# Hash attention and a gated feed-forward on one core: another order of both stages' pools, and DMA landings counted in the planned order of the queues

## Chip, cores and metric

The kernel runs on one core of a Trainium2 chip. The metric is the device time of one execution in microseconds (us), as the median of several runs. All durations of single instructions come from one profiled execution.

## What is computed

The reference is a block of attention with a hash mask, followed by a feed-forward block:

```python
q, k, v: (4, 8, 768, 64)        proj: (64, 6)
q_bucket, k_bucket = buckets of (q @ proj > 0), (k @ proj > 0)   # 6 bits each
scores = where(q_bucket == k_bucket, q @ k.T / sqrt(64), -1e9)
attn   = exp(scores - max); attn /= attn.sum(-1) + 1e-9
x      = (attn @ v) as (3072, 512)
h      = x @ w_in               # w_in (512, 2048)
out    = (h * erf(softplus(h))) @ w_out      # w_out (2048, 512)
```

## The kernel before

**Two stages.** `attention` works on 16 pairs of heads. For pair i TensorE computes the scores (line 554, 12 blocks of 384 queries by 128 keys for each of the two heads), ScalarE takes the exponential (line 581), VectorE adds blocks up for the divisor (line 627, `sum_keys`), and TensorE multiplies by v (line 639, `weigh`). `feed_forward` then takes six tiles of 512 tokens. Both of its matrix products are done as seven block products in place of eight (a scheme of Strassen's kind), so VectorE makes sums of blocks beforehand: of x (line 343, `presum_x`), of w_in (line 796, `presum_weights`) and of w_out (line 1330, `presum_w`). The first product is at line 1245, its results are copied to the tiles `h` by ScalarE (line 1263, `read`) and added to by VectorE (line 1267, `complete`), a gate of sigmoids follows (lines 1275 to 1300), and the second product is at line 1358. For the first three of its 48 steps the first product uses PSUM banks that the second product doesn't need yet (names M in the profile), later the bank X.

**The order is written by a planner.** Each stage gives its steps to `arrange` as `Op` records: engine, cost, rank, what it comes after, and `late`, the time from the end of a step until its result can be used on another engine. `arrange` runs a simple model of the engines and returns one list. The instructions are issued in that order, so each engine's queue keeps it. The planner decides only the order. What is waited for in the run is set by semaphores, which follow from the data and from the memory that tiles share.

**The way of a pair's divisor.** `divisor` (line 684, TensorE) sums over the keys, `keep_divisor` copies to `z` (ScalarE), `spread` sends z to memory (SP, zd<-z, line 724), `gather` reads it back across the partitions (SP, zc<-zd, line 731), `invert` takes the reciprocal (VectorE, lines 741 and 744), `ungather` sends it out (SP, rd<-zc, line 749), `widen` reads it back broadcast (SP, r<-rd, line 759), `normalise` multiplies (VectorE, line 770) and `send` stores x (SP, xs<-x, line 778). The last pair, number 15, does this inside the feed-forward's list (`late`), with tiles in `area`.

**The way of a pair's bits.** `bits_of` (line 842, TensorE), `sign_of` (line 851, ScalarE), `weigh_bits` (line 861, VectorE), `leave_bits` (POOL, bd<-sg, line 871), `place_bits` (POOL, both<-bd, line 880). POOL also issues the loads of the weights in pieces (`fetch_weights`, raw<-in_w, line 460), which VectorE and ScalarE convert (lines 474 to 536). Three raw buffers take turns.

**The seam between the stages.** The pools of `attention` are closed when those of `feed_forward` open, and take the same memory from the same start. A pool lies behind the one opened before it. Before the change the bytes per partition, counted from that start, are:

| stage | pools in order |
|---|---|
| attention | load 0 to 27648, bitp to 34560, ep to 53808, xst 53824 to 72256, rawp to 84544, cvt |
| feed_forward | work 0 to 32768, hp to 65536, sums to 71680, wtp to 83968, outp |

The pool xst holds the tiles x, z and r of the divisor's way. The pool hp holds the eight tiles `h`. The first product of feed-forward starts with P1 and P2 (8 matmuls each); P6, the next, writes into the bank of P1 and so follows the copy of P1 to `h` (the first line 1263), then comes P5. P6, P5, P7 and P4 take sums that `presum_x` makes from the x of tile 0, loaded by `load_x(0)` (SP, area<-xs, line 331).

Of the kernel before, what the change touches and what calls it, by code (L numbers as in the profile page):

```python
# [86 lines left out]
class Op:  # L87
# [10 lines left out]
    free: tuple = ()  # L98
    table: str = None
    late: float = 0.06  # L100


TABLE_LOAD = 1.28
# [14 lines left out]
def arrange(ops, rooms, patience=0.0):  # L118

    names = {op.name: op for op in ops}
    users, missing = {}, {}
    for op in ops:
        needs = {a for a in op.after if a in names}
        missing[op.name] = len(needs)
        for a in needs:
            users.setdefault(a, []).append(op)
    ranked = sorted(ops, key=lambda op: op.rank)
    clock = {op.engine: 0.0 for op in ranked}  # L130
    ready, released = {}, {}
    rings = {ring: [] for ring in rooms}
    open_ops = {engine: [] for engine in clock}
    table = "exp"
    order = []

    def open_up(op):
        at = 0.0
        for a in op.after:
            if a in names:  # L140
                away = 0.0 if names[a].engine == op.engine else names[a].late
                at = max(at, ready[a] + away)
        open_ops[op.engine].append((op, at))

    def start_of(op, at):
        at = max(at, clock[op.engine])
        if op.take:
            ring, room = rings[op.take[0]], rooms[op.take[0]]
            if len(ring) >= room:
                at = max(at, released.get(ring[-room], float("inf")))  # L150
        return at

    for op in ranked:
        if not missing[op.name]:
            open_up(op)
    while len(order) < len(ops):
        best = None
        for engine, entries in open_ops.items():
            starts = [(start_of(op, at), op) for op, at in entries]
            starts = [each for each in starts if each[0] < float("inf")]  # L160
            if not starts:
                continue
            first = min(start for start, _ in starts)
            start, op = min(
                (
                    (start, op)
                    for start, op in starts
                    if start <= first + (patience if op.rank[0] == 0 and engine != "PE" else 0.0)
                ),
                key=lambda each: (each[1].rank, each[0]),  # L170
            )
            if best is None or start < best[0]:
                best = start, op
        start, op = best
        end = start + op.cost
        if op.table and op.table != table:
            table = op.table
            end += TABLE_LOAD
        clock[op.engine] = ready[op.name] = end
        if op.take:  # L180
            rings[op.take[0]].append(op.take)
        for what in op.free:
            released[what] = end + op.late
        open_ops[op.engine] = [each for each in open_ops[op.engine] if each[0] is not op]
        order.append(op)
        for user in users.get(op.name, ()):
            missing[user.name] -= 1
            if not missing[user.name]:
                open_up(user)
    return order  # L190
# [3 lines left out]
def kernel(  # L194
# [14 lines left out]
    NPAIR = B * H // 2  # L209
# [4 lines left out]
    JP = NPAIR // B  # L214
# [202 lines left out]
    def attention():  # L417
        NS = NPAIR * 4
        with (
            tc.tile_pool(name="load", bufs=3) as load,  # L420
            tc.tile_pool(name="bitp", bufs=1) as bitp,
            tc.tile_pool(name="ep", bufs=1) as ep,
            tc.tile_pool(name="xst", bufs=1) as xst,
            tc.tile_pool(name="rawp", bufs=3) as rawp,
            tc.tile_pool(name="cvt", bufs=1) as cvt,
            tc.tile_pool(name="psum", bufs=1, space=PSUM) as psum,
# [394 lines left out]
            def op(fn, args, engine, cost, rank, after=(), **more):  # L821
                name = (fn.__name__,) + args
                ops.append(Op(name, engine, cost, rank, lambda: fn(*args), after=after, **more))
# [93 lines left out]
            for what, n in order:  # L917
                free = slots[-3] if len(slots) >= 3 else ()
                if what == "score":
                    i = n // 4  # L920
# [57 lines left out]
            for h in range(NH):  # L978
                i = h // 2
# [3 lines left out]
            for i in range(NPAIR):  # L983
                n = 4 * i
                if i:
                    op(
                        start_pair,
                        (i,),
                        "SP",
                        3.6,  # L990
                        (0, n - 6),
                        (("weigh", n - 9), ("bits_of", i - 1))
                        + tuple(("measure", i - 3, m, half) for m in range(2) for half in range(2)),
                        late=3.5,
                    )
                    if i == 1:
                        op(place_first, (), "ACT", 0.9, (0, n - 2, 9), (("bits_of", i),))
                        for ab in (1, 0):
                            op(weigh_first, (ab,), "DVE", 0.43, (0, n - 2, 1), (("place_first",),))
                        op(double_first, (), "DVE", 0.35, (0, n - 2, 2), (("weigh_first", 0), ("weigh_first", 1)))  # L1000
                    else:
                        op(sign_of, (i,), "ACT", 0.6, (0, n - 6, 9), (("bits_of", i), ("leave_bits", i - 1)))
                        op(weigh_bits, (i,), "DVE", 0.33, (0, n - 6, 1), (("sign_of", i),))
                        op(leave_bits, (i,), "POOL", 0.7, (0, n - 6, 2), (("weigh_bits", i),), late=3.6)
                        op(
                            place_bits,
                            (i,),
                            "POOL",
                            1.2,
                            (0, n - 6, 3),  # L1010
                            (("leave_bits", i), ("score", n - 5, 2), ("clean", i - 2)),
                            late=3.6,
                        )
                for m in range(2):
                    for half in range(2):
                        op(
                            measure,
                            (i, m, half),
                            "ACT",
                            0.65,  # L1020
                            (1, 2 * i + 2, 2 + m, half),
                            (("start_pair", i), ("score", n, 0)),
                        )
                if i == NPAIR - 1:
                    continue
                op(spread, (i,), "SP", 0.4, (0, n, 0), (("keep_divisor", i),), late=3.0)
                op(gather, (i,), "SP", 0.35, (0, n, 1), (("spread", i),), late=4.5)
                op(invert, (i,), "DVE", 0.4, (0, n + 8, 3), (("gather", i),))
                op(ungather, (i,), "SP", 0.35, (0, n, 2), (("invert", i),), late=3.0)
                op(  # L1030
                    widen,
                    (i,),
                    "SP",
                    1.1,
                    (0, n, 3),
                    (("ungather", i), ("normalise", i - 2)),
                    late=6.5,
                )
                op(normalise, (i,), "DVE", 1.02, (0, n + 8, 4), (("widen", i), ("leave", 2 * i + 1)))
                op(send, (i,), "SP", 0.35, (0, n, 4), (("normalise", i),), late=2.2)  # L1040
            for n in range(2):
                op(clean, (n,), "POOL", 1.4, (0, 4 * n), (("score", 4 * n + 3, 2),), late=0.3)
            for n in range(len(pieces)):
# [7 lines left out]
                    late=7.0,  # L1051
# [7 lines left out]
            for k in range(4):  # L1059
# [11 lines left out]
                    )  # L1071
                    + ((("sum_keys", NPAIR - 1, 2),) if k % 4 == 3 else ()),
                )
            op(load_x, (0,), "SP", 1.1, (1, 0), (("send", JP - 1), ("divisor", NPAIR - 3)), late=4.0)
            for k in range(4):
                op(presum_x, (0, k), "DVE", 0.62, (2, 31, 8 + k), (("load_x", 0), ("presum_x", 0, k - 1), ("divisor", NPAIR - 2)))
            for each in arrange(ops, {}):
# [120 lines left out]
    def feed_forward(check, late):  # L1198
        again = late is None
        with (  # L1200
            tc.tile_pool(name="work", bufs=1) as work,
            tc.tile_pool(name="hp", bufs=8) as hp,
            tc.tile_pool(name="sums", bufs=1) as sums,
            tc.tile_pool(name="wtp", bufs=2) as wtp,
            tc.tile_pool(name="outp", bufs=1) as outp,
            tc.tile_pool(name="ps_f", bufs=1, space=PSUM) as ps_f,
            tc.tile_pool(name="ps_l", bufs=1, space=PSUM) as ps_l,
        ):
# [216 lines left out]
            def op(name, engine, cost, rank, fn, args, **more):  # L1425
                ops.append(Op(name, engine, cost, rank, lambda: fn(*args), **more))
# [277 lines left out]
            if late:  # L1704
                for k, (engine, cost, name) in enumerate(
# [10 lines left out]
                        late=6.0,  # L1716
# [53 lines left out]
    with tc.manual_schedule():  # L1770
        late = attention()
        feed_forward(judge, late)
    again = nc.values_load(flag[0:1, 0:1], min_val=0, max_val=1)
    with tc.If(again > 0):
        general()
        feed_forward(None, None)
# [53 lines left out]
```

## Time and profile before

| what | value |
|---|---|
| median of 3 runs (lowest, highest) | 910.35 us (909.51, 911.08) |
| profiled execution, its own time | 910.26 us |
| span of the profile | 908.2 us, so 2.1 us lie around it |
| mean granted TensorE clock | 0.995 of full speed |
| TensorE (PE) busy | 897.4 us, 99% of the span |
| VectorE (DVE) busy | 669.5 us, 74% |
| ScalarE (ACT) busy | 563.3 us, 62% |
| GpSimd (POOL) busy | 58.3 us, 6% |

A busy figure is the sum of the instructions' durations on one engine. In the views by windows each row is a stretch of the execution, with the busy time of each engine and the number of instructions in brackets, then the granted TensorE clock, the busy share of the DMA engines and GB/s. In the views of waits a row is who waited, for whom, and then the total in us, how often, and the longest. In a timeline a row has the start, the duration, the engine and the instructions, merged where equal ones follow each other.

### The profile page before, as it was taken

What the parts mean: (1) busy time and instruction counts of PE and PEld (TensorE: products, weight loads), DVE (VectorE), ACT (ScalarE), POOL (GpSimd) and SP (SyncE); (2) the same over time, 40 slices, a digit from 0 to 9 for tenths busy, and PEclk for the clock granted to TensorE, in tenths of its full rate; (3) what the DMA queues carried; (4) which work ended last, traced back from release to release, by engine and by line L of the source; (5) the groups of instructions that cost most, each with busy time, mean ns of one, the idle gap of its engine ahead of it and who ended that gap; (6) DMA issues with size and microseconds to landing.
All of it is one profiled execution on the core that took longest, in us unless ns stands there. A gap on an engine that the chain in (4) does not pass through costs nothing.

```text
span 908.2 us, 12781 instructions
## 1 busy us (share of the span) xinstructions
PE 897.4 (99%) x5016; PEld 673.2 (74%) x5016; DVE 669.5 (74%) x837; ACT 563.3 (62%) x808; POOL 58.3 (6%) x95
## 2 busy tenths in 40 slices
PE   9999999999999999999999999999999999999997
PEld 5455554455445578888888888888888888888886
DVE  5999999999989759996666556756776556655653
ACT  7788887788876548854645545555655555545520
POOL 1211211111210000000000001000100000000000
PEclk9999999999999989999999999999999999999999
DMA  9556665656652412201032114211321123011321
GB/s 232 148 141 174 174 180 159 179 165 176 155 176 60 128 62 64 82 35 70 30 88 81 35 47 105 82 35 47 87 99 35 35 58 93 35 30 50 73 70 50
DMA packets 65156, 86.82 MB, mean 96 GB/s; under 512 B 34364, under 2 KB 47772, under 8 KB 65088
## 3 DMA queue, kind: packets, MB, share of 16 engines
q1 hardware_dynamic: 56528, 63.81, 24.4%
q0 software_dynamic: 8112, 21.66, 8.4%
q8 instruction: 41, 0.67, 0.3%
q10 hardware_dynamic: 448, 0.46, 0.2%
q14 instruction: 27, 0.22, 0.1%
HBM read 64.67 MB, written 17.30 MB: 90 GB/s over the span
## 4 chain that ended last, share of the span: by engine, by line
PE 96%; DVE 2%; DMA 1%; issue 0%; ACT 0%; SPq 0%; ACTq 0%; DVEq 0%
PE M L1358 32%; PE X L1245 29%; PE st L554 16%; PE av L639 13%; PE M L1245 3%; PE bits L842 1%; PE bits L684 1%; DMA zd<-z 1%; PE warm L804 0%; DVE area L627 0%; PE bits L374 0%; DMA xs<-x 0%; PE z_ps L684 0%; DMA zc<-zd 0%; DVE x L770 0%
## 5 line engine op out<-in xcount | busy, mean ns | idle before, releaser
L1285 DVE SCALAR_TENSOR_TENSOR e<-w,e 128x1024 f32<-128x1024 f32 x144 | 173.7, 1220 | 8.3 <-ACT w L1279 3.9
L1245 PE MATMUL X<-area,w_in_sb 128*128 128x256 f32 x680 | 160.6, 379 | 0.0
L1279 ACT ACTIVATE w<-h,cq 128x1024 f32<-128x1024 f32 x144 | 155.6, 1136 | 0.1
L554 PE MATMUL st<-q,k 64*128 64x384 f32 x768 | 155.1, 482 | 0.0
L1267 DVE TENSOR_TENSOR h<-X,h 128x512 f32<-128x512 f32 x65 | 44.8, 689 | 144.4 <-PE X L1245 144.4
L1245 PEld LDWEIGHTS X<-area,w_in_sb 128*128 128x128 f32 x680 | 129.2, 190 | 17.6
L1358 PE MATMUL M<-w_out_sb,h 128*128 128x256 f32 x576 | 141.1, 379 | 0.0
L1245 PE MATMUL X<-area 128*128 128x256 f32 x520 | 122.8, 379 | 0.0
L1358 PEld LDWEIGHTS M<-w_out_sb,h 128*128 128x128 f32 x576 | 109.4, 190 | 14.9
L1263 ACT COPY h<-X 128x512 f32<-128x512 f32 x85 | 49.3, 580 | 111.4 <-PE X L1245 111.3
L1245 PEld LDWEIGHTS X<-area 128*128 128x128 f32 x520 | 98.8, 190 | 13.4
L1275 ACT ACTIVATE e<-h,cq 128x1024 f32<-128x1024 f32 x48 | 55.1, 1149 | 85.9 <-DVE h L1267 85.8
L1358 PE MATMUL M<-wt,S 128*128 128x256 f32 x384 | 95.1, 379 | 0.0
L554 PEld LDWEIGHTS st<-q,k 64*128 64x128 f32 x768 | 68.9, 187 | 29.2 <-issue 26.5
L627 DVE TENSOR_TENSOR area<-area 128x1536 f32<-128x1536 f32 (+1 forms) x46 | 79.5, 1729 | 3.5 <-ACT area L581 1.4
L1358 PEld LDWEIGHTS M<-wt,S 128*128 128x128 f32 x384 | 73.0, 190 | 9.9
L581 ACT ACTIVATE e_even<-st 128x768 f32<-128x768 f32 x96 | 70.5, 823 | 0.3 <-PE st L554 0.3
L581 ACT ACTIVATE area<-st 128x768 f32<-128x768 f32 x90 | 67.8, 817 | 0.0
L639 PE MATMUL av<-e_even,v 128*64 128x385 f32 x384 | 65.6, 490 | 0.0
L554 PE MATMUL st<-both 64*128 64x384 bf16 x384 | 63.6, 323 | 0.3 <-ACT both L387 0.3
L1300 DVE TENSOR_TENSOR h<-h,e 128x1024 f32<-128x1024 f32 x48 | 57.9, 1220 | 4.6 <-ACT e L1296 4.6
L639 PE MATMUL av<-area,v 128*64 128x384 f32 x360 | 60.6, 486 | 0.0
(129 smaller groups left out, 981.8 us busy)
## 6 DMA issues: line engine op xcount, KB each, us to landing
wt<-wt SPq DMA_DIRECT2D x24, 768.0 KB, 4.3
raw<-in_w_out_dram POOLq DMA_DIRECT2D x16, 512.0 KB, 4.7
raw<-in_w_in_dram POOLq DMA_DIRECT2D x14, 512.0 KB, 4.6
v<-in_v_dram SPq DMA_DIRECT2D x32, 192.0 KB, 3.9
q<-in_qkT_dram SPq DMA_DIRECT2D x30, 192.0 KB, 4.0
k<-in_qkT_dram SPq DMA_DIRECT2D x30, 192.0 KB, 4.4
r<-rd SPq DMA_DIRECT2D x30, 192.0 KB, 3.5
xs<-x SPq DMA_DIRECT2D x15, 384.0 KB, 2.8
```

What stands on the lines that cost most here:

```text
L554: nc.tensor.matmul(out=st[:, ab, 0:HS], lhsT=d["k" + src][rows, keys], rhs=d["q" + src][rows, cols], start=(part == 0), stop=(part == 1),)
L581: nc.scalar.activation(out=e[:, :, 0:HS], in_=st[:, :, 0:HS], func=AF.Exp, scale=scale)
L627: nc.vector.tensor_tensor(out=into, in0=one, in1=two, op=ALU.add)
L639: nc.tensor.matmul(out=d["av", half][rows, 0:w], lhsT=d["v"][:, g * GC + c, rows], rhs=e[:, ab, 0:w], start=(g == 0 and c == 0), stop=(g = ...
L1245: nc.tensor.matmul(out=d[where][:, u, :], lhsT=a[:, kc, f : f + P], rhs=b[:, kc, :], start=(first and u == 0 and kc == 0), stop=(last and ...
L1263: nc.scalar.copy(out=quarter(p, q), in_=st[p][where])
L1267: nc.vector.tensor_tensor(out=h, in0=st[p][where], in1=h, op=ALU.add)
L1275: nc.scalar.activation(out=s, in_=unit(p, v), func=AF.Sigmoid, bias=cq[:, n : n + 1])
L1279: nc.scalar.activation(out=q, in_=unit(p, v), func=AF.Sigmoid, scale=GATE_S[j][0], bias=cq[:, j : j + 1])
L1285: nc.vector.scalar_tensor_tensor(out=s, in0=st[p].pop(("q", v, j)), scalar=GATE_S[j][2], in1=s, op0=ALU.add, op1=ALU.mult,)
L1300: nc.vector.tensor_tensor(out=h, in0=h, in1=st[p].pop(("s", v)), op=ALU.mult)
L1358: nc.tensor.matmul(out=banks[name][:, sub, :], lhsT=a[:, u, sub * P : (sub + 1) * P], rhs=b[:, u, :], start=(c == 0 and k == 0), stop=(c = ...
```

## The change

It has four parts.

1. In `attention` the pool xst is opened after load and ahead of bitp and ep. In `feed_forward` the pools outp and sums are opened after work and ahead of hp and wtp. The sizes stay.
2. `Op` gets `far` and `near`. A step with `far=True` has its `late` counted for a user on the same engine too, unless the user names it in `near`. It is set for `leave_bits`, `spread`, `gather` and `ungather`, each followed by another transfer of the same queue that needs its data.
3. The values of `late` move: `leave_bits` 3.6 to 4.0, `spread` 3.0 to 3.5, `widen` 6.5 to 5.0.
4. `load_x(0)` comes after `gather` of pair 14 in place of `divisor` of pair 13, with `late` 6.5 in place of 4.0.

```diff
@@ class Op
     late: float = 0.06
+    far: bool = False
+    near: tuple = ()
@@ arrange, open_up
-                away = 0.0 if names[a].engine == op.engine else names[a].late
+                near = names[a].engine == op.engine and (not names[a].far or a in op.near)
+                away = 0.0 if near else names[a].late
@@ attention
             tc.tile_pool(name="load", bufs=3) as load,
+            tc.tile_pool(name="xst", bufs=1) as xst,
             tc.tile_pool(name="bitp", bufs=1) as bitp,
             tc.tile_pool(name="ep", bufs=1) as ep,
-            tc.tile_pool(name="xst", bufs=1) as xst,
@@
-    op(leave_bits, (i,), "POOL", 0.7, (0, n - 6, 2), (("weigh_bits", i),), late=3.6)
+    op(leave_bits, (i,), "POOL", 0.7, (0, n - 6, 2), (("weigh_bits", i),), late=4.0, far=True)
@@
-    op(spread, (i,), "SP", 0.4, (0, n, 0), (("keep_divisor", i),), late=3.0)
-    op(gather, (i,), "SP", 0.35, (0, n, 1), (("spread", i),), late=4.5)
+    op(spread, (i,), "SP", 0.4, (0, n, 0), (("keep_divisor", i),), late=3.5, far=True)
+    op(gather, (i,), "SP", 0.35, (0, n, 1), (("spread", i),), late=4.5, far=True)
     op(invert, (i,), "DVE", 0.4, (0, n + 8, 3), (("gather", i),))
-    op(ungather, (i,), "SP", 0.35, (0, n, 2), (("invert", i),), late=3.0)
+    op(ungather, (i,), "SP", 0.35, (0, n, 2), (("invert", i),), late=3.0, far=True)
@@ widen
-                    late=6.5,
+                    late=5.0,
@@
-    op(load_x, (0,), "SP", 1.1, (1, 0), (("send", JP - 1), ("divisor", NPAIR - 3)), late=4.0)
+    op(load_x, (0,), "SP", 1.1, (1, 0), (("send", JP - 1), ("gather", NPAIR - 2)), late=6.5, near=(("gather", NPAIR - 2),))
@@ feed_forward
             tc.tile_pool(name="work", bufs=1) as work,
+            tc.tile_pool(name="outp", bufs=1) as outp,
+            tc.tile_pool(name="sums", bufs=1) as sums,
             tc.tile_pool(name="hp", bufs=8) as hp,
-            tc.tile_pool(name="sums", bufs=1) as sums,
             tc.tile_pool(name="wtp", bufs=2) as wtp,
-            tc.tile_pool(name="outp", bufs=1) as outp,
```

## The prediction

> **What bounds the kernel now.** I read the engines' shares first, then who TensorE waits for, then the granted clock by stretches around the only long wait, and last the chain that leads into that wait. The page's first part:
>
> ```profile
> PE 897.4 (99%) x5016; PEld 673.2 (74%) x5016; DVE 669.5 (74%) x837; ACT 563.3 (62%) x808; POOL 58.3 (6%) x95
> ```
>
> TensorE is the bound. So only TensorE's idle time and its slow time can be won. All its waits, from the view of waits for PE:
>
> ```profile
> PE M L1245 <- ACT h L1263: 2.9, 1, 2.9
> PE warm L804 <- DVE ones L250: 1.0, 1, 1.0
> PE M L1245 <- DVE h L1267: 0.7, 1, 0.7
> PE st L554 <- ACT both L387: 0.3, 1, 0.3
> ```
>
> One wait matters: 2.9 us, once, in the first product of feed-forward, for the copy of a result to `h`. The windows around it, with the clock behind the bracketed counts:
>
> ```profile
> 313.43:317.15 3.72, 3.72 (x18) 2.96 (x16) 3.72 (x5) 0.48 (x1) 0.00 (x0) 1.00 0.40 134
> 317.15:320.09 2.94, 0.00 (x1) 0.00 (x0) 2.39 (x4) 0.59 (x1) 0.00 (x0) 0.85 0.34 134
> 320.09:326.65 6.56, 6.56 (x16) 5.04 (x17) 1.97 (x4) 0.59 (x1) 0.00 (x0) 0.55 0.30 121
> 326.65:347.70 21.05, 20.39 (x109) 17.02 (x109) 16.06 (x25) 14.45 (x18) 0.00 (x0) 1.00 0.09 26
> ```
>
> The reader is to see the third row: a "busy" TensorE that does 16 matmuls in 6.56 us, where 8 take 1.73 us later (a row of the long chain: `358.82 1.73 PE X L1245 x8`). The wait costs twice, as idle time and as a slow clock after it. Cut finer:
>
> ```profile
> 319.00:319.20 0.20, 0.00 (x0) 0.00 (x0) 0.20 (x1) 0.00 (x0) 0.00 (x0) 0.96 0.00 0
> 319.20:319.40 0.20, 0.00 (x0) 0.00 (x0) 0.20 (x1) 0.00 (x0) 0.00 (x0) 0.50 0.00 0
> 325.80:326.00 0.20, 0.20 (x2) 0.20 (x1) 0.00 (x0) 0.00 (x0) 0.00 (x0) 0.50 0.00 0
> 326.00:326.20 0.20, 0.20 (x3) 0.17 (x2) 0.00 (x0) 0.00 (x0) 0.00 (x0) 0.97 0.00 0
> ```
>
> The clock halves about 2.0 us after TensorE's last modelled end (317.15) and returns 5.9 us after it starts again. The chain of waits over this stretch says what the copy waited for:
>
> ```profile
> 315.49 1.02 DVE x L770
> 316.50 0.02 issue
> 316.52 2.30 DMA xs<-x
> ...
> 319.45 0.60 ACT h L1263
> 320.05 0.04 issue
> 320.09 6.63 PE M L1245 x16
> ```
>
> The copy of P1 could have started when P1's matmuls ended, near 315.4 (313.43 plus 8 matmuls, 1.73, plus about 0.2). It started at 319.45, behind the store of the last x that `normalise` made. No data joins them. What joins them is memory: hp covers bytes 32768 to 65536, and the tiles x lie at 53824 to 63040, in xst. The first tile h lies at 32768 to 36864 and touches no x, so the wait holds for the pool as a whole. The view of the tile x agrees (who waited for it: `ACT h L1263: 5.4, 1`).
>
> **What the skill says.** The Trainium skill, "TensorE: Matmul & The Clock Gate", Part 1: The HAM clock gate, says that TensorE's clock is halved after an idle window and restored after a busy one, and that the windows (about 3.4 us) run freely. The trace agrees on the half (0.50), with 2.0 us of idle time and 5.9 us of work around it. So a remaining wait under some 2 us need not halve the clock: the 0.66 us wait at 344.31 did not (clock 1.00 from 339 to 345). "DMA: Bandwidth & Descriptors", Issuing engines are not separate DMA queues, says that transfers of SP and POOL share the same engines. That bears on the reordered transfers; the trace has the DMA engines busy 0.56 of the time from 27.3 to 318.9.
>
> **The change part by part.**
>
> *Pools.* By the sizes in front of the reader, xst now lies at 27648 to 46080, bitp to 52992, ep to 72240. In feed-forward outp lies at 32768 to 45056, sums to 51200, hp at 51200 to 83968. So hp lies over both1, junk, e_even and the raw buffers, and no longer over x, z or r. What the first copy to `h` must now wait for: the exponentials' sums over e_even (DVE, done by about 304), the last squares into junk (ACT, 307.7 in the trace), the bits of pair 15 (landed by 287.4) and P1 itself. P1 is last. xst is now under work, outp and sums. Their first writers are the sigmoid at line 1275 (331.92 before, some 326 after), line 1315 and the output, all after the last store has landed (316.52 + 2.30 = 318.8). The four L1330, which waited 0.5 us for the store, are freed too. Price of the pools elsewhere: nothing, since no instruction changes its shape.
>
> *The gain.* From the start of P1 to the start of the next kind of work (z_ps, line 684) the trace has 326.65 - 313.43 = 13.22 us. The same 32 matmuls at 1.73 us per 8 take 6.92, and the changeover about 0.1. The gain is 13.22 - 7.0 = **6.2 us**: some 3.1 of idle time and 3.1 of half clock.
>
> *Does it last?* From 347.7 to 862 TensorE is busy 514.30 of 514.30 us, so whatever starts sooner ends sooner. Between 326.65 and 347.7 the order on TensorE, ScalarE and VectorE is the same in both programs, and everything there follows from TensorE's results. VectorE could be late instead: before, it idles 7.48 us ahead of line 1267 at 329.54. With TensorE 6.2 us sooner that line comes at 323.3. VectorE's work before it (the end of attention near 316.2 as worked out below, 2.5 for four L1330, 0.7 for the first line 1267) ends near 319.4, so 3.9 us are left. What is late next is the 0.66 us wait at 344.31, which stays.
>
> *The list.* TensorE's order is the same instruction for instruction. On SP `send` of pair i-1 now stands between `spread` and `gather` of pair i; before it stood ahead of both. At the end of attention, SP has spread 13, spread 14, send 12, gather 13, gather 14, load_x, ungather 13 and 14, widen 13 and 14. Worked out: `invert` of pair 12 comes one sum later (286.62 + 1.7 = 288.3), its r lands near 294.5, `normalise` 12 ends near 298, so send 12 goes at 298, the gathers at about 299, load_x at 299.7. In the trace load_x took from 295.42 to 301.28, 5.9 us, so x is there at 305.6. VectorE starts the last pair's sums at 300.3 (fourth exponential); 1.75 + 1.70 + 0.96 of sums, 0.8 of inverting, 1.23 at line 796, 1.9 of sums bring the first `presum_x` to 308.6 and the second, which P6 needs, to an end at 309.9. P6 could start at 316.9: 7 us to spare. The last sums end near 314.2 and `normalise` near 316.2, against 316.5 before. All of this lies beside TensorE. I take nothing for it. The bounds: not below nothing, since TensorE waits for none of this work now, and +1.5 above, the case of rival 1.
>
> *POOL.* One or two fetches (0.57 us each to issue) now stand between `leave_bits` and `place_bits`. The tightest pair before:
>
> ```profile
> 203.66 0.55 POOL L871 DMA_DIRECT2D bd<-sg  x1 [15.22 <-DVE sg L861]
> 208.99 1.16 POOL L880 DMA_DIRECT2D both<-bd  x2 [4.78 <-DMA bd<-sg]
> ```
>
> It lands 2.1 us later, at 212.25, and the scores that read it start at 219.23: 7.0 us of slack. A fetch fills the time in which POOL waited anyway (4.78 us). Sharing engines with a 512 KB piece costs at most its 4.7 us. I take nothing.
>
> The sum: 910.26 - 6.2 = 904.06 for the profiled execution, whose own time is 0.09 under the median. Prediction **904.1 us**.
>
> **Rivals.**
>
> 1. *A shorter wait takes its place.* P6 then waits for `presum_x`, as load_x stands behind the gathers and send 12. For: SP is strictly in order, and `normalise` 12 waits for a chain of four transfers. Against: 7 us of slack. If it comes 1.5 us too late the clock stays up: 904.1 + 1.5 = 905.6.
> 2. *The same loss by another way.* x lands 10 us later than worked out, P6 waits 3 us and the clock halves again: 910.3, no change. A form of it is that the pool still waits for the store by another tile; against it speaks that hp and xst no longer share a byte.
> 3. *Slower: bits too late.* A fetch stuck on a raw buffer holds `place_bits` on POOL. Its buffer is freed by a conversion on VectorE, 0.42 + 0.69 + 0.69 + 0.43 + 0.69 + 0.69 = 3.6 us, and ahead of it can stand a pair's five sums, 8.7 us. That is 12.3 us, 5.3 beyond the slack, and the idle TensorE then pays the half clock as well (3.1): 8.4 for each pair hit, 904.1 + 8.4 = 912.5 with one pair, 921 with two. It decides from a delay of 7 us. For: VectorE is busy 270.6 of 291.6 us in this stage. Against: on VectorE the conversion that frees the buffer stands ahead of the `weigh_bits` for which `leave_bits` has waited, in all but the earliest pair.
>
> **How the numbers follow.** The measurement can tell 0.2% (1.8 us) from no change. Forecast 0.87, rival 1 0.05, rival 2 0.04, rival 3 0.04. The forecast's own range is 903.2 to 905.2 (the runs before spread by 0.8 to each side, the gain by 0.3). Taken up to rival 1, and down for the 0.66 us wait at 344.31 going too, the range is 902.8 to 906.0. Faster 0.92, same 0.04, slower 0.04.
>
> **What would show it.** Right: no row "PE M L1245 <- ACT h" over 0.3 us, a clock of 1.00 from 313 to 345, the first copy to `h` near 315.5, z_ps near 320.4 in place of 326.65, and a span near 902. Wrong: a halved clock after 313, a wait of PE for `area` at line 343, or a wait of the scores for `both` with POOL behind a raw buffer.

## The result, and the profile after

| | median | lowest to highest | runs |
|---|---|---|---|
| before | 909.51 us | 907.82 to 911.08 | 5 |
| after | 904.56 us | 904.18 to 904.86 | 5 |

The ratio is 0.9945 (95% interval 0.993 to 0.9959): faster by about 5 us. The profiled execution of after took 904.72 us, with a span of 902.9 and a mean granted clock of 0.998 (before 910.26, 908.2 and 0.995). In the changed file every line touched here stands three lines lower, so L1263 is now L1266.

TensorE's waits in the kernel after, from the view of waits (who, for whom, then total, times, longest):

```profile
PE warm L807 <- DVE ones L253: 1.0, 1, 1.0
PE M L1248 <- DVE h L1270: 0.7, 1, 0.7
PE st L557 <- ACT both L390: 0.3, 1, 0.3
```

The 2.9 us row is gone and the three others are as they were. The timeline of TensorE at the seam of the two stages, after:

```profile
313.46 3.72 PE L1248 MATMUL M<-area,w_in_sb 128*128 128x256 f32 x16
317.02 3.62 PE L1248 MATMUL M<-area 128*128 128x256 f32 x16
320.56 0.86 PE L687 MATMUL z_ps<-area,ones 128*32 128x192 f32 x16
...
338.22 3.72 PE L1248 MATMUL M<-area,w_in_sb 128*128 128x256 f32 x16 [0.66 <-DVE h L1270]
```

The second row is P6 and P5. They follow P1 and P2 without a gap and take 3.62 us where they took 6.63. The windows over the same stretch give the granted clock, the third number from the end, as 1.00:

```profile
313.46:317.02 3.56, 3.56 (x19) 3.15 (x17) 3.51 (x5) 1.07 (x2) 0.00 (x0) 1.00 0.23 91
317.02:320.56 3.54, 3.54 (x17) 2.85 (x15) 2.40 (x4) 0.59 (x1) 0.00 (x0) 1.00 0.60 240
```

From P1 to `z_ps` there are now 320.56 - 313.46 = 7.10 us, against 13.22: 6.12 less, and the last matmul of the program ends 6.09 sooner (896.20 for 902.29). The span shrank by only 5.3, since the end behind the last matmul took 6.7 us in this execution and 5.9 in that of before. The timeline of all engines after, around the moved steps:

```profile
297.65 0.42 SPq L781 DMA_DIRECT2D xs<-x  x1
299.12 0.46 SPq L334 DMA_DIRECT2D area<-xs  x1
...
308.48 1.41 DVE L346 TENSOR_TENSOR area<-area 128x512 f32<-128x512 f32 x2
...
314.35 1.94 DVE L773 SCALAR_TENSOR_TENSOR x<-x,ev,r 128x768 f32<-128x768 f32 x2
315.38 1.25 SPq L781 DMA_DIRECT2D xs<-x  x2
315.61 0.59 ACT L1266 COPY h<-M 128x512 f32<-128x512 f32 x1 [1.56 <-PE M L1248]
...
323.45 0.69 DVE L1270 TENSOR_TENSOR h<-M,h 128x512 f32<-128x512 f32 x1 [4.03 <-PE M L1248]
```

The two stores of x in the row at 315.38 are issued at 315.38 and 316.31. The first copy to `h` starts at 315.61, so 0.70 us before the last store is even issued: it waits for TensorE, no longer for a store.

### The profile page after: what moved, and what is told of

Its sections match the earlier page's. It is cut to its first block, busy times and chain, and to the rows that moved or that the text cites. A ratio compares the mean times of both kernels' runs of the same rounds, so it can differ in the third digit from the quotient of the medians.

```text
span 902.9 us, 12780 instructions
## 1 busy us (share of the span) xinstructions
PE 894.3 (99%) x5016; PEld 670.9 (74%) x5016; DVE 668.5 (74%) x837; ACT 563.3 (62%) x808; POOL 57.9 (6%) x95
## 4 chain that ended last, share of the span: by engine, by line
PE 99%; DVE 0%; issue 0%; ACT 0%; DVEq 0%
PE M L1361 32%; PE X L1248 29%; PE st L557 17%; PE av L642 14%; PE M L1248 3%; PE bits L845 1%; PE bits L687 1%; PE warm L807 0%; PE bits L377 0%; PE z_ps L687 0%; DVE e L1288 0%; DVE h L1270 0%; ACT both L390 0%; DVE u L1396 0%; DVE norms L1754 0%
## 5 line engine op out<-in xcount | busy, mean ns | idle before, releaser
L1270 DVE TENSOR_TENSOR h<-X,h 128x512 f32<-128x512 f32 x65 | 44.8, 689 | 144.4 <-PE X L1248 144.4
L1266 ACT COPY h<-X 128x512 f32<-128x512 f32 x85 | 49.3, 580 | 111.4 <-PE X L1248 111.3
```

The lines of the kernel that those rows point to most:

```text
L1266: nc.scalar.copy(out=quarter(p, q), in_=st[p][where])
L1270: nc.vector.tensor_tensor(out=h, in0=st[p][where], in1=h, op=ALU.add)
```

## The experiments

The edits are given in short form here: a line that starts with # is a remark, and only what matters of each line is kept. In brackets behind a measured time stand its ratio to before and the 95% interval of the ratio.

**Two edits alone (e1, e2).** Both pool orders without the list's edits, and the list's edits without the pools. The list's edits are parts 2 to 4 of the change:

```diff
 # e1: before, and
-  pools load, bitp, ep, xst   /  work, hp, sums, wtp, outp
+  pools load, xst, bitp, ep   /  work, outp, sums, hp, wtp
 # e2: after, with the two pool orders of before
```

> The kernel before with the two pool orders of the change alone; every queue's order stays that of before. My theory (the whole gain is the wait of the first copy to h, and the slow clock after it): the copy starts at once after P1, the clock stays at 1.00, z_ps starts near 320.5, time 904.5 us, within 0.5 of the changed kernel. Rival (the list shares in the gain, because the sums of x or the stores come sooner with it): a wait of TensorE of 0.5 to 3 us stays at P6, time 905 to 910 us.

> The changed kernel with both pool orders of before: only the order of the queues is changed. My theory: the first copy to h waits for the last store of x as before. That store goes out some 0.2 us sooner, so the wait shrinks by 0.2 us at most, the clock is halved again, and the time is that of before, 909 to 910 us. Rival (the list carries part of the gain): 905 to 908 us.

Measured beside the same runs of before (910.95 us): pools 906.41 (ratio 0.9962, 0.9948 to 0.9975), list 910.96 (1.0004, 0.9994 to 1.0013). The list alone gives nothing; its profile has the old stall, from the timeline of TensorE of the list alone:

```profile
320.31 6.74 PE L1248 MATMUL M<-area 128*128 128x256 f32 x16 [3.05 <-ACT h L1266]
```

The pools remove it, but stop 1.8 us short of the 904.56 that the whole change had in another comparison. The expectation of 904.5 us was missed, and its rival did not come either: P6 has no wait, and P1 to `z_ps` takes 7.10 us as in the kernel after. In the profile of the pools alone VectorE stands still where the divisors come back, and TensorE has two short waits in the stage of attention. The timeline there:

```profile
193.85 0.17 DVE L741 TENSOR_SCALAR zc<-zc 128x12 f32<-128x12 f32 x1 [2.61 <-DMA zc<-zd]
...
194.21 5.35 DVE L627 TENSOR_TENSOR area<-area 128x1536 f32<-128x1536 f32 x3
...
199.48 0.15 DVE L711 TENSOR_SCALAR ev<-av 128x1 f32<-128x1 f32 x1
...
202.23 0.34 PE L554 MATMUL st<-both 64*128 64x384 bf16 x2 [0.56 <-ACT z L695]
...
203.56 0.34 PE L554 MATMUL st<-both 64*128 64x384 bf16 x2 [0.34 <-ACT e_even L581]
```

and the same pair in the kernel after:

```profile
193.85 0.17 DVE L744 TENSOR_SCALAR zc<-zc 128x12 f32<-128x12 f32 x1
...
194.19 1.70 DVE L630 TENSOR_TENSOR area<-area 128x1536 f32<-128x1536 f32 x1
...
195.80 0.15 DVE L714 TENSOR_SCALAR ev<-av 128x1 f32<-128x1 f32 x1
```

With the old list the reciprocal stands at the head of VectorE for 2.61 us, and three sums come after it, so `ev` is 3.7 us later. With the new list two of those sums ran ahead of the reciprocal. That VectorE's stop causes TensorE's two waits is likely from their order in time, and not shown. This became a second question, which the last experiment answers.

**Fill the wait with work (e3).** The kernel before, with matmuls into a spare bank between P2 and P6, so that TensorE doesn't idle while the copy waits:

```diff
+  fill_wait: 7 matmuls 128x256 from w_in_sb into the bank "dummy"
   P6: after P1's copy
+      and after fill_wait
```

> The kernel before with seven matmuls added behind P2 (14 in the records, some 3.0 us), whose result nobody reads: the wait stays, but TensorE is busy in it. My theory (about half of the loss is the halved clock and not the wait): P6 still starts near 320.1, the clock stays at 1.00, P6 and P5 take 3.5 us in place of 6.6, time 3.1 us under before, near 906.4 us, and the spread over the runs of before (3.3 us) shrinks to that of the changed kernel (0.7 us). Rival (the 6.6 us are due to something else, such as the operands or the banks of P6 and P5): no gain, 909.5 us.

Measured 908.67 (0.9981, 0.9971 to 0.9992). The timeline of TensorE:

```profile
317.22 3.19 PE L1428 MATMUL dummy<-w_in_sb 128*128 128x256 f32 x14
320.66 3.72 PE L1245 MATMUL M<-area 128*128 128x256 f32 x16 [0.25 <-ACT h L1263]
324.31 0.86 PE L684 MATMUL z_ps<-area,ones 128*32 128x192 f32 x16
```

P6 starts no sooner than before (320.66 for 320.09), and yet P6 and P5 take 3.72 us in place of 6.63, at a granted clock of 1.00. P1 to `z_ps` takes 10.65 us in place of 13.22. So 2.57 of the 6.12 us that the stall cost there were not the wait but the clock after it. Two parts of the expectation failed: the median fell by 2.3 us and not by 3.1, and the runs still spread over 3.25 us (907.38 to 910.63).

**The remaining 0.66 us (e4).** The changed kernel with the matmuls of the norms' bound (line 1746) at an earlier place of the list:

```diff
-  check: rank (0, 1, 9),   after P3, late
+  check: rank (0, 0, 5.5), after P3, late, complete(0, 3)
```

> The changed kernel with the check of the bound (the small matmuls of line 1746 and the reductions on VectorE) taken ahead of P4 of the first step, into VectorE's idle time near 323 to 325, in place of after the first step. My theory (TensorE's one remaining wait of 0.66 us at 338.2 is VectorE's work in front of line 1270): the wait goes, and the time falls by up to 0.6 us to 903.9 us; 0.1 to 0.3 us may come back as P3's sum on VectorE is later. Rival (that wait has another cause): no change.

Measured 904.02 (0.9938, 0.9925 to 0.995), 0.54 under the changed kernel's median in the first comparison; the wait for L1270 has left the list of TensorE's waits. It is the fastest version of this study, by less than the two spreads allow to be sure of (903.77 to 904.55 against 904.18 to 904.86).

**One half of the pools at a time (e5, e6).** The kernel before with xst moved in `attention` alone, and with outp and sums moved in `feed_forward` alone:

```diff
 # e5
-  load, bitp, ep, xst
+  load, xst, bitp, ep
 # e6
-  work, hp, sums, wtp, outp
+  work, outp, sums, hp, wtp
```

> The kernel before with xst moved in attention alone. By the bytes, hp (32768 to 65536) then still covers the end of xst (27648 to 46080): two of the three x tiles, z and r. My theory (the copy waits for every tile under the whole of its pool): the wait for the store stays, time as before, 909 to 911 us. Rival (a copy waits only for what lies under its own tile, or moving xst is the whole of the change): about 904.5 us.

> The kernel before with outp and sums moved in feed-forward alone. hp (51200 to 83968) then covers all of xst (53824 to 72256). My theory: the wait for the store stays, time as before, 909 to 911 us. Rival (moving hp is the whole of the change): about 904.5 us.

Before had 910.41; e5 909.86 (0.9991, 0.9979 to 1.0003), e6 909.57 (0.9988, 0.9979 to 0.9998). Either half keeps the wait, 3.03 us with the first and 2.80 with the second. In both the timeline names VectorE's line 1330 as what the copy waited for, but the chain leads through the last store of x. The chain, feed-forward pools alone:

```profile
318.40 2.31 DMA xs<-x
...
320.93 0.59 ACT h L1263
```

e5 can't tell a wait for the whole pool from one for the bytes under the tile itself, although its expectation takes it so: in the program as built its first tile h (32768 to 36864) lies over the x of pairs 13 and 14 (30720 to 36864), the last two to be stored. e6 can. Its first tile h lies at 51200 to 55296, of the x tiles over that of pair 12 alone, and its copy still starts behind the store of pair 14, whose x lies at 56896 to 59968. The timeline of TensorE, feed-forward pools alone:

```profile
321.56 5.41 PE L1245 MATMUL M<-area 128*128 128x256 f32 x16 [2.80 <-ACT h L1263]
326.90 0.86 PE L684 MATMUL z_ps<-area,ones 128*32 128x192 f32 x16
```

Here P6 and P5 take 5.41 us, between 3.6 and 6.7. The clock is at half only from about 321.7 to 325.0.

**A wait of a chosen length (e7, e8).** The changed kernel with the first copy to `h` done 5 and 8 times over, so that P6 waits for ScalarE and for nothing else:

```diff
-  nc.scalar.copy(out=quarter(p, q), in_=st[p][where])
+  for _ in range(5 if p == 0 and q == 0 and not again else 1):   # the second kernel: 8
+      nc.scalar.copy(out=quarter(p, q), in_=st[p][where])
```

> The changed kernel with the first copy to h done five times over on ScalarE, the same data each time, so that P6 waits about 1.5 us. My theory (the clock is halved only after some 2 us of idle TensorE): the wait costs itself alone, 1.5 us, time 906.1 us. Rival (any wait over 1 us brings the half clock): 906.1 + 3 = 909 us.

> As the run with five copies, with eight, so that P6 waits about 3.2 us. My theory: the clock halves near 2.0 us into the wait and the same 32 matmuls lose another 3.1 us, as in the kernel before: 904.6 + 3.2 + 3.1 = 910.9 us. Rival (the half clock of before came from something else than the wait): 907.8 us.

Measured 906.77 (0.9954, 0.9936 to 0.9972) and 910.09 (0.9998, 0.9988 to 1.0007), beside 910.41 for before. The timelines of TensorE, first with 5 copies:

```profile
319.37 3.72 PE L1248 MATMUL M<-area 128*128 128x256 f32 x16 [1.54 <-ACT h L1267]
```

and with 8:

```profile
320.41 5.41 PE L1248 MATMUL M<-area 128*128 128x256 f32 x16 [3.39 <-ACT h L1267]
325.75 0.86 PE L687 MATMUL z_ps<-area,ones 128*32 128x192 f32 x16
```

1.5 us of waiting leaves the clock alone. 3.4 us brings the old time back, with the new pools and the new list in place. In the profile the wait is 0.45 us longer than in before and P6 and P5 lose 1.7 us to the clock in place of 3.1. So a wait with the clock behind it explains the old time, whatever it is that causes the wait.

**What is the list worth (e9 to e12)?** Four kernels beside the same runs of before: the changed kernel again (e9), the pools alone again (e10), the pools with the spacing of the divisors' transfers (e11), and the change without that spacing (e12):

```diff
 # e11 has of the list's edits these alone; e12 has all but these
-  spread late=3.0, gather late=4.5, ungather late=3.0, widen late=6.5
+  spread late=3.5 far, gather late=4.5 far, ungather late=3.0 far, widen late=5.0
```

> The changed kernel as it is, beside the three others of this call and the same runs of the kernel before. My prediction took the list's edits at nothing; pools alone then measured 906.4 where the changed kernel had 904.6, but in two different comparisons. If the list is worth nothing (the prediction's term) all four kernels of this call lie within 0.4 us of each other. If the list takes away small stalls of the attention stage, this kernel stays at 904.3 to 904.9 and pools alone at 905.9 to 906.9.

> Both pool orders, the list as before. Theory (small stalls): 905.9 to 906.9, 1.3 to 2.3 us above the whole change, with VectorE waiting over 5 us in all for the divisors' load (zc<-zd) and 2 us for their widened form (r<-rd), and TensorE with one or two waits of 0.3 to 1.5 us in the attention stage, not always at the same place. List worth nothing: 904.3 to 904.9.

> Both pool orders, and of the list only the spacing of the divisors' transfers on SP (spread, gather, ungather, widen); load_x and leave_bits stay as in the kernel before. Theory (VectorE's waits for the divisors are what stalls TensorE): 904.4 to 905.2, and VectorE's waits for zc<-zd and r<-rd are gone; its one wait of 2.6 us for area<-xs stays and costs nothing. Rival (the place of load_x, with VectorE's 2.6 us wait for it near 300, is what costs): 905.9 to 906.9.

> The changed kernel without the spacing of the divisors' transfers (spread, gather, ungather, widen as before); load_x and leave_bits as changed. Theory (divisors): 905.7 to 906.9, VectorE's waits for zc<-zd (over 5 us in all) back. Rival (load_x): 904.4 to 905.2, though the waits for zc<-zd are back.

| kernel | spacing | median | lowest to highest | ratio to before (909.66), interval |
|---|---|---|---|---|
| whole change (e9) | yes | 904.62 | 904.03 to 905.28 | 0.9943, 0.9928 to 0.9957 |
| pools and spacing (e11) | yes | 904.85 | 904.09 to 906.29 | 0.9947, 0.9933 to 0.9961 |
| pools alone (e10) | no | 905.91 | 905.25 to 907.43 | 0.9963, 0.9949 to 0.9978 |
| all but the spacing (e12) | no | 906.08 | 905.78 to 907.32 | 0.9962, 0.9948 to 0.9976 |

The ten runs with the spacing have a median of 904.7, the ten without it 906.0; nine of the first lie at or under 905.34, nine of the second at or over 905.64. The spacing is worth about 1.3 us, and the place of `load_x` and the edit of `leave_bits` nothing that shows. VectorE's waits for DMAs in the pools alone (second time):

```profile
DVE zc L741 <- DMA zc<-zd: 5.4, 3, 2.7
...
DVE x L770 <- DMA r<-rd: 2.7, 3, 1.3
DVE area L343 <- DMA area<-xs: 2.7, 1, 2.7
```

With the pools and the spacing the first two rows are gone, and the wait for the loaded x stays and is even longer:

```profile
DVE area L346 <- DMA area<-xs: 3.6, 1, 3.6
```

That kernel is as quick as the whole change, so VectorE's wait for `load_x` costs nothing that shows, and what counts is the spacing. In the kernel with all but the spacing the first two waits are back, 7.0 us for zc and 4.0 for r.

How the 1.3 us reach the end is not shown. From the start of `z_ps` at the seam to the last matmul it takes 575.6 us in all fourteen profiles but that of e4 (574.9), so they arise ahead of it or behind the last matmul.

- Ahead of it, the first profile of the pools alone has 0.9 us of waits of TensorE in attention, and that of the feed-forward pools alone has one of 1.5 us (`z_ps` for VectorE's sums, at 296.56). Against what was expected, the profiles of e10 and e12 have none there. Their matmuls even end sooner (895.93 and 896.18) than those of e9 and e11 with the spacing (896.76 and 896.81).
- Behind it, the end is longer in e10 and e12 (7.2 and 7.8 us) than in e9 and e11 (6.6 and 6.7). But in all fourteen profiles this end lies between 5.9 and 8.0 us without following the list (5.9 with the old one in before, 8.0 with the new one in e2).

These profiles can't settle it, since the profiled executions of e9, e10 and e11 took the same time (905.25 to 905.34 us). Nor does the new list gain anything beside the old pools (e2, 910.96 for 910.95, with an interval that leaves no room for 1.3 us). Whether TensorE's waits strike some executions and not others, or the end of the program makes the difference, stays open.

## Why the prediction was right, and where it was not

- **TensorE is the bound, and one wait is to be won: right.** What was won at the seam came through to the last matmul: 6.09 us sooner there, for 6.12 at the seam.
- **The wait is one of memory, of the pool as a whole: right.** Nothing of the data changed, and the wait went with the pools' places. Both moves are needed, as e5 and e6 show. That it is the pool and not the tile's own bytes rests on the addresses in before and in e6, where the tile h and the last x share none.
- **The wait costs twice: right, and shown three ways.** Work put into the wait keeps the clock up (e3), 1.5 us of waiting keep it up (e7), and 3.4 us of waiting for another cause bring the old time back (e8).
- **The gain of 6.2 us: right for the profiled pair, too large for the median.** The pools alone moved the medians by 4.5 us (e1) and 3.75 us (e10), the whole change by 4.95 and 5.04. The term that was mis-sized is "3.1 of half clock". It was read from one execution, which showed the longer of two cases. The half clock lasted 6.8 us in the profiles of before (319.2 to 326.0), e2 and e5, at a loss of 3.1 us, and 3.4 us in those of e6 and e8 (about 321.7 to 325.0), at a loss of 5.41 - 3.72 = 1.7. In the median it is worth some 2.3 us: that is what e3 saved. The runs of before agree with a mixture. Of the 50 in the comparison of e5 to e8, 12 had a mean clock of 0.995 and a median of 911.5, 24 one of 0.996 or 0.997 and 910.4, 14 one of 0.998 or more and 908.7. A half clock of 3.4 us takes 1.7 / 908 = 0.0019 off the mean clock, and one of 6.8 us 0.0037. These runs have no trace, and in the fourteen profiles the half clock behind the last matmul takes another 0.001 to 0.003 off, so that reading is argued. Why the pools alone stay under the whole change is the open question of the last experiment.
- **The list, "I take nothing for it": wrong by 1.3 us.** The prediction asked which waits of TensorE the list could add, and bounded it at "not below nothing, since TensorE waits for none of this work now". That was true of one execution. With the new pools the list came out below nothing, as a gain. The waits of before had VectorE waiting 5.5 us for zc and 2.1 for r, and these were passed over; that they are the cause is not shown. The two errors offset each other: some 4 us from the pools and 1.3 from the list, in place of 6.2 and 0. So it is in part luck that 904.1 came within 0.5 us of 904.56.
- **The times of the moved steps: right within 0.9 us.** `send` of pair 12 at 297.65 (298 worked out), the first gather at 298.17 (about 299), `load_x` at 299.12 (299.7), the second sum of x ending at 309.89 (309.9), the last `normalise` ending at 316.29 (316.2), line 1270 at 323.45 with 4.03 us of idle time ahead of it (323.3 and 3.9). The 0.66 us wait stayed. None of the three rivals came about. One reading on POOL was wrong without effect: "at most its 4.7 us" for a 512 KB piece is the median, and the longest took 7.5.

## What to carry to other kernels

When a busy engine waits once for something without any data in common, compare the addresses of the pools on both sides of the stage's border: a wait for a whole pool goes when the late writer's memory falls to a tile that is needed later. Price such a stall as the idle time and the slow clock behind it, the latter as a range and not as the value of one execution. And an edit that only touches waits of a second engine is not worth nothing because the first engine happened not to wait in the one profile at hand: compare several runs before it is put at nothing.

## What the hardware showed

- The Trainium skill, "TensorE: Matmul & The Clock Gate", Part 1: The HAM clock gate, says that the activity window is 3413 ns long and runs freely. The half clock at the seam lasted 3.4 or 6.8 us in five profiles, one or two such windows, which agrees. The same section has the clock halved after an idle window of about 3.4 us. Here less was enough: in before it was halved 2.0 us after the last matmul's modelled end. That delay varied: some 2.0 us in before, about 3.4 behind the end of the program's matmuls in after, and some 4.6 in e8 (317.02 to 321.66), where TensorE had been at work again for 1.25 us when its clock was halved. The windows of the kernel with 8 copies, with the clock third from the end:

```profile
317.00:320.41 3.41, 0.02 (x1) 0.00 (x0) 1.66 (x3) 3.20 (x6) 0.00 (x0) 1.00 0.59 238
...
321.60:321.80 0.20, 0.20 (x2) 0.20 (x1) 0.00 (x0) 0.00 (x0) 0.00 (x0) 0.66 0.00 0
324.80:325.00 0.20, 0.20 (x2) 0.11 (x2) 0.00 (x0) 0.00 (x0) 0.00 (x0) 0.50 0.00 0
325.00:325.20 0.20, 0.20 (x2) 0.20 (x1) 0.00 (x0) 0.00 (x0) 0.00 (x0) 0.81 0.00 0
```

- Which of the two lengths came went with what TensorE did when its clock was halved. In before, e2 and e5 it still stood idle (halved at 319.18, 319.62 and 319.64, P6 at 320.09, 320.31 and 320.38), and the half clock lasted 6.8 us. In e6 and e8 it was back at work (halved at 321.64 and 321.66, P6 at 321.56 and 320.41), and the half clock lasted 3.4 us. That would follow if the clock came back only after one whole window of work: in the first three TensorE idled another 0.7 to 0.9 us after the halving. Five profiles agree with it, and no run was made to test it. The moment of halving, first in e5 and then in e6:

```profile
319.60:319.80 0.20, 0.00 (x0) 0.00 (x0) 0.20 (x1) 0.06 (x1) 0.00 (x0) 0.61 0.00 0
...
321.60:321.80 0.20, 0.20 (x1) 0.20 (x2) 0.20 (x1) 0.00 (x0) 0.00 (x0) 0.61 0.00 0
```

- The kernels with the half clock mostly spread more, but the cause of the spread is not shown. Before ran from 907.55 to 914.56 us over the 50 runs beside e5 to e8, and only from 909.53 to 910.42 over the 8 beside e9 to e12. The changed kernel ran from 904.03 to 905.28 over its ten runs. And e3, with no half clock at the seam of its profile, still spread over 3.25 us.
